# Batch 0 of a Fourier-mixing and mixture-of-experts kernel stays on chip between its stages

## The chip, the cores and the metric

The kernel runs on one core of one Trainium2 chip. The metric is the device time of one execution in microseconds (us), the median of several. A profile of one execution gives a span from the first to the last instruction, which is a little shorter than such a time. The engines are called TensorE (PE in the profile; PEld is its weight load), VectorE (DVE), ScalarE (ACT), GpSimd (POOL) and SyncE (SP, which here issues most transfers).

## What is computed

Two blocks follow each other, all in fp32. The first mixes each of 8 batches of 2496 x 256 along the sequence with a filter in the Fourier domain:

```python
X = np.fft.rfft(x, axis=1)
Y = X * (filt_r + 1j * filt_i)[None, :, :]
y = np.fft.irfft(Y, n=x.shape[1], axis=1)
```

The second takes the 19968 rows of y as tokens, sends each to the one expert of 8 with the largest logit, and scales the expert's result by the softmax weight of that expert:

```python
logits = x @ w_gate
expert_idx = np.argmax(logits, axis=1)
h = np.maximum(x_sorted[lo:hi] @ w1[e], 0.0)      # 256 -> 1024
y_sorted[lo:hi] = h @ w2[e]                        # 1024 -> 256
out = gate_w[:, None] * y_sorted[inv_perm]
```

No token is dropped, so the number of rows of each expert is known only at run time.

## The kernel before

**The Fourier block** splits 2496 = 39 x 64 and runs in four stages, each a set of small matmuls against a table. Stage A (`stage_a`, L324 to L335) transforms over the 39 with table `tas`; three columns of 39 make 117 partitions, and 22 such groups of columns are taken two at a time in chunks of four (`CH`). Its result z goes to DRAM (`zd`), because stage B needs the other index on the partitions. Stage B (`stage_b`, L337 to L354) transforms over the 64 for one pair of the 20 frequencies f with table `tbs`, and multiplies by the filter `ht` on VectorE with four operations (L350 to L353). Stage C (`stage_c`) goes back over the 64 with table `tcs`, and its result u goes through DRAM (`ud`) for the same reason. Stage D (`stage_d`, L377 to L391) goes back over the 39 with table `tds`, and leaves rows y.

**Routing.** `turn_y` transposes y, `logits` multiplies by `w_gate`, `turn_logits` transposes back, and `route` (L431 to L541), in three groups for each batch, finds the expert, and counts with two small matmuls into the PSUM tile `rk` (L467, L468) which row of the expert's list each token takes. GpSimd then scatters the rows to a list in DRAM (L526). `route` is a generator: each `yield` lets the main loop go on with something else.

**Experts.** `tile_map` reads from the counts which tiles of 512, 256 or 128 rows can be worked on. For each tile the rows are loaded (`xg`), transposed (`turn_x`), multiplied by `w1` (`hidden`, L663) with a ReLU, multiplied by `w2` (`result`, L677), scaled, and scattered to the output by GpSimd (L683).

**Order.** The order of the instructions on TensorE, VectorE, ScalarE and SyncE is written out by the kernel's own main loop, which keeps a clock `now` of planned costs. `slot(k)` lists the steps of one slot with a place between 0 and 1 for each: stages B and C of batch k, stage A of batch k+1, stage D and routing of batch k-1. Ahead of slot 0 stand stage A of batch 0 and the loads of the filter tables, in turn. After each step of the Fourier block the loop issues stores (`flush`) and loads that have room (`more_loads`, seven input buffers), and calls `side()` twice, each of which runs the routing to its next `yield`. Expert steps come in between when their data are planned to be there. `evac` copies a PSUM bank to SBUF on VectorE or ScalarE, whichever is planned to be free first; so all these copies have the line L231.

Each engine works in order: an instruction that waits holds up all that stand behind it on that engine.

Of the kernel before, what the change touches and what calls it, by code (L numbers as in the profile page):

```python
# [10 lines left out]
F32 = mybir.dt.float32  # L11
# [16 lines left out]
NF = (N1 + 1) // 2  # L28

NB = 3  # L30
NG = 22
TP = NB * N1
DH = D // P
# [3 lines left out]
def dft_tables():  # L37

    w = 2.0 * np.pi
    q = np.arange(N1)
    t = np.arange(N2)
    g = np.arange(N2)
    half = N2 // 2
    sg = np.where(g < half, 1.0, -1.0)  # L50

    ta = np.zeros((NB, N1, NB, N1))
    for f in range(NF):
        ang = w * ((q * f) % N1) / N1
        for j in range(NB):
            ta[j, :, j, f] = np.cos(ang)
            if f:
                ta[j, :, j, NF - 1 + f] = -np.sin(ang)

    tb = np.zeros((2, N2, NF, 2, N2))  # L60
    for f in range(NF):
        ang = w * ((t[:, None] * (f + N1 * g)[None, :]) % S) / S
        c, sn = np.cos(ang), np.sin(ang)
        if f:
            tb[0, :, f, 0] = c
            tb[1, :, f, 0] = sn
            tb[0, :, f, 1] = -sn * sg
            tb[1, :, f, 1] = c * sg
        else:
            tb[0, :, f, 0, :half] = c[:, :half]  # L70
            tb[0, :, f, 1, 1:half] = -sn[:, 1:half]
            tb[0, :, f, 0, half] = (-1.0) ** t

    tc = np.zeros((2, N2, 2, 2, N2))
    ang = w * ((g[:, None] * t[None, :]) % N2) / N2
    c, sn = np.cos(ang), np.sin(ang)
    tc[0, :, 1, 0] = c
    tc[0, :, 1, 1] = sn
    tc[1, :, 1, 0] = -sn * sg[:, None]
    tc[1, :, 1, 1] = c * sg[:, None]  # L80
    tc[0, :half, 0, 0] = 2.0 * c[:half]
    tc[1, :half, 0, 0] = -2.0 * sn[:half]
    tc[1, 0, 0, 0] = 0.0
    tc[0, 0, 0, 0] = 1.0
    tc[0, half, 0, 0] = (-1.0) ** t

    td = np.zeros((NB, N1, NG, NB, N1))
    ids = np.zeros((NB, N1, NG))
    valid = np.zeros((NB, N1, NG))
    for j in range(NB):  # L90
        for i in range(len(range(j, N2, NB))):
            n = N2 * q + NB * i + j
            ids[j, :, i] = n
            valid[j, :, i] = 1.0
            td[j, 0, i, j] = 1.0 / S
            for f in range(1, NF):
                ang = w * ((n * f) % S) / S
                td[j, f, i, j] = 2.0 / S * np.cos(ang)
                td[j, NF - 1 + f, i, j] = -2.0 / S * np.sin(ang)

    return {
        "ta": ta.reshape(TP, TP),
        "tb": tb.reshape(P, NF, P),
        "tc": tc.reshape(P, 2, P),
        "td": td.reshape(TP, NG, TP),
        "ids": ids.reshape(TP, NG),
        "valid": valid.reshape(TP, NG),
    }
# [24 lines left out]
def kernel(  # L133
# [37 lines left out]
    zd = [dram.tile([N2, N1, D], F32, tag=f"z{b % 2}", name="zd") for b in range(B)]  # L171
    ud = [dram.tile([N2, N1, D], F32, tag=f"u{b % 2}", name="ud") for b in range(B)]
# [13 lines left out]
    moe = ctx.enter_context(tc.tile_pool(name="moe", bufs=2))  # L186
# [7 lines left out]
    tas = cst.tile([TP, TP], F32, name="tas")  # L194
    tbs = cst.tile([P, NF, P], F32, name="tbs")
    tcs = cst.tile([P, 2, P], F32, name="tcs")
    tds = cst.tile([TP, NG, TP], F32, name="tds")
# [12 lines left out]
    tau_i = cst.tile([1, 64], I32, name="tau_i")  # L210

# [31 lines left out]
    def load_filters(c):  # L243
        f0, n = FH[c]
        nc.sync.dma_start(out=tbs[:, f0:f0 + n], in_=tb[:, f0:f0 + n])
        nc.sync.dma_start(out=ht[:, f0:f0 + n], in_=filt[:, f0:f0 + n, :])
        if c == 0:
            nc.sync.dma_start(out=ht[:, NF:], in_=filt[:, NF:, :])
            nc.sync.dma_start(out=tcs, in_=tcm)
# [28 lines left out]
    def columns(ap, i0, n):  # L278

        rows = ap.rearrange("t s d -> (t s) d")  # L280
        m = min(n, NG - 1 - i0)
        yield TP, slice(0, m), rows[i0 * TP:(i0 + m) * TP, :].rearrange("(i p) d -> p i d", p=TP)
        if m < n:
            yield N1, slice(m, n), rows[(NG - 1) * TP:, :].rearrange("(i p) d -> p i d", p=N1)
# [6 lines left out]
    def move(o, i):  # L291
        moves[1].append(lambda: nc.sync.dma_start(out=o, in_=i))
# [18 lines left out]
    def load_z(b, c):  # L311
        f0, n = FH[c]
        z0 = 1 if f0 == 0 else 0
        zi = fin(("z", b, c))
        nc.sync.dma_start(out=zi[:HP, :n], in_=zd[b][:, f0:f0 + n, :])
        nc.sync.dma_start(out=zi[HP:, z0:n], in_=zd[b][:, NF - 1 + f0 + z0:NF - 1 + f0 + n, :])
# [7 lines left out]
    def stage_a(b, c):  # L324
        i0, n = CH[c]
        xt = ins.pop(("x", b, c))
        zo = sb.tile([TP, 4, D], F32, tag="st", name="zo", bufs=4)
        for j in range(0, n, 2):
            p = bank()
            mm(p[:TP, :], lhsT=tas, rhs=xt[:TP, j:j + 2, :], start=True, stop=True)  # L330
            evac(zo[:, j:j + 2, :], p[:TP, :].rearrange("p (t d) -> p t d", t=2), 512)
        for r, m, v in columns(zd[b], i0, n):
            move(v, zo[:r, m])
        if c == len(CH) - 1:
            mark(("a", b))  # L335

    def stage_b(b, f):  # L337
        c, j = divmod(f, 4)
        zi = ins["z", b, c] if j == 0 else ins.pop(("z", b, c))
        p = bank()  # L340
        for i in range(2):
            k = HP if f + i == 0 else P
            mm(p[:, i * D:(i + 1) * D], lhsT=tbs[:k, f + i, :], rhs=zi[:k, j + i, :], start=True, stop=True)  # L343
# [9 lines left out]
        nc.vector.tensor_tensor(ys, ys, yw, op=ALU.add)  # L353
        free["v"] = max(free["v"], now[0]) + 2.8  # L354

    def stage_c(b, f):
# [12 lines left out]
        if j == 2:  # L369
            f0 = f - 2  # L370
            z0 = 1 if f0 == 0 else 0
            move(ud[b][:, f0:f0 + 4, :], uo[:HP])
            move(ud[b][:, NF - 1 + f0 + z0:NF - 1 + f0 + 4, :], uo[HP:, z0:])
# [3 lines left out]
    def stage_d(b, c):  # L377
# [4 lines left out]
        ui = ins.pop(("u", b, c))  # L382
        yo = outs["o", b, c] = sb.tile([P, 4, DR], F32, tag="y", name="yo", bufs=6)[:TP]
        for j in range(0, n, 2):
            p = bank()
            for i in range(2):

                k = N1 if i0 + j + i == NG - 1 else TP
                mm(p[:TP, i * D:(i + 1) * D], lhsT=tds[:k, i0 + j + i, :], rhs=ui[:k, j + i, :],  # L389
                   start=True, stop=True)  # L390
            evac(yo[:, j:j + 2, :D], p[:TP, :].rearrange("p (i d) -> p i d", i=2), 512)  # L391

# [38 lines left out]
    def route(b, g):  # L431
# [32 lines left out]
        yield  # L464
        rk = psr.tile([P, 2, E * NG], F32, tag="rk", name="rk")
# [78 lines left out]
    def tile_map(b, rows, n, last):  # L544

        av_i = moe.tile([1, E], I32, name="av_i", bufs=1)
        av = moe.tile([1, E], F32, name="av", bufs=1)
        end = moe.tile([1, E], F32, name="end", bufs=1)
# [9 lines left out]
        base = moe.tile([1, E], F32, name="base", bufs=1)  # L558
        add = moe.tile([1, E], F32, name="add", bufs=1)
# [6 lines left out]
        tau = moe.tile([1, n], F32, tag=f"tau{n}", name="tau", bufs=1)  # L566
        past = moe.tile([1, n, E - 1], F32, tag=f"past{n}", name="past", bufs=1)
# [5 lines left out]
        ef = moe.tile([1, n], F32, tag=f"ef{n}", name="ef", bufs=1)  # L573
        erow = moe.tile([1, n], I32, tag=f"erow{n}", name="erow", bufs=2)
# [4 lines left out]
        rf = moe.tile([1, n], F32, tag=f"rf{n}", name="rf", bufs=1)  # L579
        rrow = moe.tile([1, n], I32, tag=f"rrow{n}", name="rrow", bufs=2)  # L580
# [3 lines left out]
        if last:  # L584

            stop = moe.tile([1, 1], F32, name="stop", bufs=1)
# [5 lines left out]
        if not last:  # L592

            take = moe.tile([1, E], F32, name="take", bufs=1)
# [17 lines left out]
    def rows_in(i):  # L612
# [3 lines left out]
        xg = xgs[i] = moe.tile([P, 4, DR], F32, tag="xg", name="xg")  # L616
# [10 lines left out]
    def weights(h, second):  # L627
# [10 lines left out]
        if second:  # L638
            w2t[h] = moe.tile([P, FH2, D], F32, tag="w2t", name="w2t", bufs=3)
            nc.sync.dma_start(out=w2t[h], in_=moe_w2[bass.ds(ev, 1), k].rearrange("o p i d -> p (o i) d"))  # L640
        else:
            pool, bufs = (late["w1"], 8) if i >= SHORT else (moe, 3)
# [3 lines left out]
    def turn_x(i):  # L646
        n, xg = work[i][0], xgs.pop(i)
        idt[i] = moe.tile([P, 4, 1], I32, tag="idt", name="idt", bufs=3)
        gts[i] = moe.tile([P, 4, 1], F32, tag="gts", name="gts", bufs=3)
        nc.vector.tensor_copy(idt[i][:, :n], xg.bitcast(I32)[:, :n, D:D + 1])  # L650
        nc.vector.tensor_copy(gts[i][:, :n], xg[:, :n, D + 8:D + 9])
        xts[i] = moe.tile([P, DH, 4 * P], F32, tag="xT", name="xT", bufs=1)
# [6 lines left out]
    def hidden(i, k):  # L659
# [5 lines left out]
        hT = moe.tile([P, 512], F32, tag="hT", name="hT", bufs=9)  # L665
# [4 lines left out]
    def result(i, j):  # L670
# [7 lines left out]
        ys = moe.tile([P, D], F32, tag="ys", name="ys", bufs=4)  # L678
# [16 lines left out]
    def slot(k):  # L695

        steps, nch = [], len(CH)
        if k < B:
# [9 lines left out]
        if k > 0:  # L708
            for c in range(nch + 3):
                at = 0.2 + 0.8 * c / (nch + 3)  # L710
                if c < nch:
                    steps.append((at, lambda c=c: stage_d(k - 1, c), ("u", k - 1, c), 0.43 * CH[c][1]))
# [7 lines left out]
            steps.append((2.0, lambda: begin_route(k - 1), None, 0.0))  # L720
        return sorted(steps, key=lambda step: step[0])

    STEPS = []
    for c in range(len(CH)):
        STEPS.append((0.0, lambda c=c: stage_a(0, c), ("x", 0, c), 0.43 * CH[c][1]))
        if c < len(FH):
            STEPS.append((0.0, lambda c=c: load_filters(c), None, 0.0))
    STEPS.append((0.0, load_rest, None, 0.0))
# [12 lines left out]
    todo = [step[2] for step in STEPS if step[2]]  # L741
# [75 lines left out]
    with tc.manual_schedule(  # L817
# [8 lines left out]
        while f or e:  # L826
            asked = e and e[2] in when

            halt = f and f[2] and f[2][0] == "u" and held_y[0] == 6
# [5 lines left out]
            elif f and not halt and (not f[2] or f[2] in ins):  # L835
# [9 lines left out]
            side()  # L845
            side()
# [37 lines left out]
```

## Time and profile before

| what | value |
|---|---|
| time, median of 3 | 1698.14 us (1694.24 to 1699.72) |
| span of the profiled execution | 1670.8 us |
| mean granted TensorE clock | 0.974 |
| first stage-B matmul starts | 40.0 us |
| first stage-D matmul starts | 90.1 us |
| first expert matmul (L663) starts | 203.1 us |
| moved from and to DRAM | 299 MB, 179 GB/s over the span |

In the profile, L with a number is a line of the kernel. A group of instructions is written out<-in by the names in the program. A wait names the engine and the tile that waited, then what released it, then the total, the number of times and the longest in us. "issue" is time in which the profile shows nothing that the engine waited for. A matmul of fp32 appears as two records, one for each pass.

### The profile page before, as it was taken

The numbers are of one execution on the slowest core, as the hardware profiler recorded it, in microseconds if no ns is written. First come the engines' busy times: TensorE is split into PE (matmuls) and PEld (weight loads), VectorE is DVE, ScalarE is ACT, GpSimd is POOL, SyncE is SP. The second block draws the span as 40 slices with busy tenths as digits, with TensorE's granted clock in tenths as the row PEclk, the third lists the DMA queues.
The fourth block names the chain that finished last, engine by engine and source line by source line (L and its number), as shares of the span: only waits on it lengthen the run. The fifth ranks groups of instructions, "written<-read, shape, count | busy, mean of one in ns | idle before, by whom it ended". The sixth has DMA issues, their size and how long they took to land.

```text
span 1670.8 us, 21186 instructions
## 1 busy us (share of the span) xinstructions
PE 1574.8 (94%) x6886; PEld 1125.5 (67%) x6886; DVE 617.6 (37%) x1921; ACT 325.1 (19%) x608; POOL 344.3 (21%) x363
## 2 busy tenths in 40 slices
PE   3888798999999999999999989999999999999998
PEld 1454465677666666666676666676767668889997
DVE  0766776454632243233533332221101003334443
ACT  1333232121222222212222212212111110000000
POOL 0003322312410232021412221341111111111111
PEclk7899899999999999999999999999999999999999
DMA  8888887676673547434744353443344446565561
GB/s 318 272 242 266 255 265 239 205 256 184 213 244 115 168 154 231 150 121 126 197 134 129 121 160 101 129 152 121 109 158 143 145 140 224 190 207 174 176 189 47
DMA packets 125429, 299.53 MB, mean 179 GB/s; under 512 B 17681, under 2 KB 62874, under 8 KB 125075
## 3 DMA queue, kind: packets, MB, share of 16 engines
q1 hardware_dynamic: 106104, 254.85, 49.3%
q0 software_dynamic: 19216, 43.33, 7.6%
q8 instruction: 56, 0.92, 0.2%
q14 instruction: 53, 0.43, 0.1%
HBM read 213.91 MB, written 85.10 MB: 179 GB/s over the span
## 4 chain that ended last, share of the span: by engine, by line
PE 87%; DVE 6%; DMA 4%; issue 2%; ACT 0%; SPq 0%; POOLq 0%; POOL 0%; DVEq 0%; ACTq 0%
PE bank L677 33%; PE bank L663 33%; PE bank L389 4%; PE bank L330 3%; PE bank L367 3%; PE bank L343 3%; DMA zd<-zo 2%; PE bank L656 2%; PE bank L399 2%; PE lt L413 1%; DVE yw L352 1%; DVE yw L351 1%; DVE ys L350 1%; DVE ys L353 1%; DMA ud<-uo 1%
## 5 line engine op out<-in xcount | busy, mean ns | idle before, releaser
L663 PE MATMUL bank<-xT,w1t 128*128 128x512 f32 (+2 forms) x2080 | 590.9, 436 | 0.8 <-ACT xT L231 0.8
L677 PE MATMUL bank<-w2t,hT 128*128 128x256 f32 x2240 | 500.0, 380 | 0.0
L663 PEld LDWEIGHTS bank<-xT,w1t 128*128 128x128 f32 x2080 | 338.6, 191 | 203.7 <-issue 182.5
L677 PEld LDWEIGHTS bank<-w2t,hT 128*128 128x128 f32 x2240 | 423.3, 191 | 64.1 <-issue 9.4
L683 POOL DMA_INDIRECT out_dram<-ys,idt x163 | 159.5, 978 | 942.0 <-DVE ys L681 420.1
L526 POOL DMA_INDIRECT rows<-yo,row x176 | 175.4, 996 | 377.1 <-issue 225.5
L667 ACT ACTIVATE hT<-bank 128x512 f32<-128x512 f32 (+1 forms) x241 | 140.3, 582 | 494.2 <-PE bank L663 494.2
L681 DVE TENSOR_SCALAR ys<-bank,gts 128x256 f32<-128x256 f32 x145 | 70.1, 484 | 429.5 <-PE bank L677 429.5
L666 DVE TENSOR_SCALAR hT<-bank 128x128 f32<-128x128 f32 (+1 forms) x279 | 94.0, 337 | 70.2 <-PE bank L663 70.2
L343 PE MATMUL bank<-fin,tbs 128*128 128x256 f32 (+1 forms) x320 | 88.6, 399 | 23.6 <-issue 23.0
L330 PE MATMUL bank<-fin,tas 117*117 117x512 f32 x176 | 94.4, 665 | 6.0 <-DMA fin<-in_x_dram 5.9
L343 PEld LDWEIGHTS bank<-fin,tbs 128*128 128x128 f32 (+1 forms) x320 | 60.1, 198 | 55.9 <-issue 45.9
L389 PE MATMUL bank<-fin,tds 117*117 117x256 f32 (+1 forms) x352 | 88.7, 392 | 6.6 <-DMA fin<-ud 6.6
L231 DVE COPY xT<-bank 128x512 f32<-128x512 f32 (+2 forms) x59 | 28.3, 480 | 162.8 <-ACT hT L667 98.2
L350 DVE TENSOR_TENSOR ys<-bank,ht 128x512 f32<-128x512 f32 x80 | 55.0, 688 | 87.7 <-PE bank L343 86.3
L389 PEld LDWEIGHTS bank<-fin,tds 117*117 117x117 f32 (+1 forms) x352 | 64.5, 187 | 33.7 <-issue 14.0
L367 PE MATMUL bank<-ys,tcs 128*128 128x512 f32 x144 | 78.8, 630 | 8.0 <-DVE ys L353 8.0
L231 ACT COPY xT<-bank 128x512 f32<-128x512 f32 (+2 forms) x71 | 29.9, 431 | 284.3 <-PE bank L656 200.9
L677 PE MATMUL bank<-w2s,hT 128*128 x368 | 83.2, 379 | 0.0
L677 PEld LDWEIGHTS bank<-w2s,hT 128*128 128x128 f32 x368 | 68.2, 190 | 8.2
L231 ACT COPY uo<-bank 128x512 f32<-128x512 f32 x80 | 46.9, 586 | 119.3 <-PE bank L367 91.3
L330 PEld LDWEIGHTS bank<-fin,tas 117*117 117x117 f32 x176 | 35.0, 203 | 42.4 <-issue 37.5
(106 smaller groups left out, 852.0 us busy)
## 6 DMA issues: line engine op xcount, KB each, us to landing
w1t<-in_moe_w_dram SPq DMA_DIRECT2D x130, 512.0 KB
w2t<-in_moe_w_dram SPq DMA_DIRECT2D x84, 512.0 KB
fin<-in_x_dram SPq DMA_DIRECT2D x40, 512.0 KB
zd<-zo SPq DMA_DIRECT2D x40, 468.0 KB
fin<-ud SPq DMA_DIRECT2D x40, 468.0 KB
fin<-zd SPq DMA_DIRECT2D x72, 256.0 KB
ud<-uo SPq DMA_DIRECT2D x72, 256.0 KB
xg<-rows SPq DMA_DIRECT2D x28, 544.0 KB
```

The costliest lines, as they stand in the source:

```text
L231: either(n, lambda: nc.vector.tensor_copy(o, i), lambda: nc.scalar.copy(out=o, in_=i))
L330: mm(p[:TP, :], lhsT=tas, rhs=xt[:TP, j:j + 2, :], start=True, stop=True)
L343: mm(p[:, i * D:(i + 1) * D], lhsT=tbs[:k, f + i, :], rhs=zi[:k, j + i, :], start=True, stop=True)
L350: nc.vector.tensor_mul(ys, z2, ht[:, f:f + 2, :])
L367: mm(p, lhsT=tcs[:, 1, :], rhs=ys, start=True, stop=True)
L389: mm(p[:TP, i * D:(i + 1) * D], lhsT=tds[:k, i0 + j + i, :], rhs=ui[:k, j + i, :], start=True, stop=True)
L526: sc = nc.gpsimd.indirect_dma_start(out=rowsd, out_offset=bass.IndirectOffsetOnAxis(ap=at, axis=0), in_=what, in_offset=None,)
L663: mm(p[:, :m], lhsT=w1t[2 * i + k // FH2][:, dh, k % FH2 * P:(k % FH2 + 1) * P], rhs=xts[i][:, dh, :m], start=(dh == 0), stop=(dh == DH - 1))
L666: either(m, lambda: nc.vector.tensor_scalar_max(hT[:, :m], p[:, :m], 0.0), lambda: nc.scalar.activation(hT[:, :m], p[:, :m], AF.Relu))
L667: lambda: nc.scalar.activation(hT[:, :m], p[:, :m], AF.Relu))
L677: mm(p[:, :D], lhsT=hs[i][k][:, j * P:(j + 1) * P], rhs=w2, start=(k == 0), stop=(k == FT - 1))
L683: nc.gpsimd.indirect_dma_start(out=out, out_offset=bass.IndirectOffsetOnAxis(ap=idt[i].bitcast(U32)[:, j, :], axis=0), in_=ys, in_offset=None,
```

## The change

Batch 0 is the first through all stages, and nothing else is there to be done while it goes through DRAM. The changed kernel keeps it in SBUF. Stage A of batch 0 (`first_a`) has the data as the weights and the table as the moving operand, so that z comes out with the model dimension on the partitions; it is kept in the tile `zt`. `turn_z` transposes the part that stage B needs for a pair of frequencies. Stage C (`first_c`) does the same with the tile `ut`, and `turn_u` transposes ahead of stage D. These tiles lie in a pool `pro` whose memory is given to the experts' buffers once stage D of batch 0 is planned (`experts_pool`). For this a place is added so that z and u have 40 columns instead of 39 (`NS`), also for the other batches. For batch 0 the last of the four operations of stage B is given to GpSimd.

The filter tables are loaded ahead of all stores; the real part, which was loaded twice, once for each half of the partitions, is loaded once and copied on ScalarE. Stage D of batch 0 is placed early in slot 1. In `route` the rank product is placed ten yields later, and the main loop calls `side()` four times after a step.

```diff
+NS = 2 * NF
+TK = NB * NS
@@ load_filters
-        nc.sync.dma_start(out=ht[:, f0:f0 + n], in_=filt[:, f0:f0 + n, :])
+        nc.sync.dma_start(out=ht[:HP, f0:f0 + n], in_=filt[:HP, f0:f0 + n, :])
+        nc.sync.dma_start(out=ht[rows, NF + f1:NF + f1 + nh], in_=filt[rows, NF + f1:NF + f1 + nh, :])
@@ stage_b
-        zi = ins["z", b, c] if j == 0 else ins.pop(("z", b, c))
+        if b == 0:
+            zi, j = outs.pop(("zi", f)), 0
+        else:
+            zi = ins["z", b, c] if j == 0 else ins.pop(("z", b, c))
...
-        nc.vector.tensor_tensor(ys, ys, yw, op=ALU.add)
+        (nc.gpsimd if b == 0 else nc.vector).tensor_tensor(ys, ys, yw, op=ALU.add)
@@ stage_d
-        ui = ins.pop(("u", b, c))
+        ui = turn_u(c) if b == 0 else ins.pop(("u", b, c))
@@ new
+    def first_a(c):
+            zu["z"] = pro.tile([P, DH, NF, 2, N2], F32, name="zt", bufs=1)
+            zu["u"] = pro.tile([P, DH, N2, 2, NF], F32, name="ut", bufs=1)
+        for j in range(0, n, 2):
+            p = bank()[:, :4 * TK]
+            for h in range(DH):
+                for i in range(2):
+                    mm(p[:, (2 * h + i) * TK:(2 * h + i + 1) * TK], lhsT=xt[:TP, j + i, h * P:(h + 1) * P], rhs=tas,
+                       start=True, stop=True)
...
+            for h in range(DH):
+                evac(zv[:, h], pv[:, h], 2 * TK)
+    def turn_z(f):
+        if f % 4 == 0:
+            nc.scalar.copy(out=ht[HP:, f:f + 4], in_=ht[:HP, f:f + 4])
...
+                nc.tensor.transpose(p[:, i, h, :], zu["z"][:, h, f + i].rearrange("p c t -> p (c t)"), ident)
+        evac(zi, p.rearrange("p i h d -> p i (h d)"), 2 * D)
+    def first_c(f):
...
+                mm(p[:, h, i].rearrange("p c t -> p (c t)"), lhsT=ys[:, i, h * P:(h + 1) * P],
+                   rhs=tcs[:, min(f + i, 1), :], start=True, stop=True)
+        for h in range(DH):
+            evac(zu["u"][:, h, :, :, f:f + 2], p[:, h].rearrange("p i c t -> p t c i"), D)
+    def turn_u(c):
+        ui = pro.tile([P, 4, D], F32, tag="ui", name="ui", bufs=1)
...
@@ route
+        for _ in range(10):
+            yield
         rk = psr.tile([P, 2, E * NG], F32, tag="rk", name="rk")
@@ slot
+        if k == 0:
+            steps.append((0.4, load_rest, None, 0.0))
...
-                at = 0.2 + 0.8 * c / (nch + 3)
+                at = 0.45 * c / (nch + 3) - 0.1 if k == 1 else 0.2 + 0.8 * c / (nch + 3)
...
+                if k == 1 and c == nch:
+                    steps.append((at, experts_pool, None, 0.0))
-            steps.append((2.0, lambda: begin_route(k - 1), None, 0.0))
+            steps.append((0.34 if k == 1 else 2.0, lambda: begin_route(k - 1), None, 0.0))
@@ STEPS
+    STEPS = [(0.0, lambda c=c: load_filters(c), None, 0.0) for c in range(len(FH))]
+    STEPS += [(0.0, lambda c=c: first_a(c), ("x", 0, c), 0.43 * CH[c][1]) for c in range(len(CH))]
@@ main loop
-            side()
-            side()
+            for _ in range(4):
+                side()
```

## The prediction

> **What bounds the kernel now.** I read the page's busy times and slices first, then a table of six stretches, the waits of TensorE, the chain of waits of the first 50 us, and TensorE's timeline at two places.
>
> The page, engine totals, granted clock and DMA share in 40 slices:
>
> ```profile
> PE 1574.8 (94%) x6886; PEld 1125.5 (67%) x6886; DVE 617.6 (37%) x1921; ACT 325.1 (19%) x608; POOL 344.3 (21%) x363
> ...
> PE   3888798999999999999999989999999999999998
> ...
> PEclk7899899999999999999999999999999999999999
> DMA  8888887676673547434744353443344446565561
> ```
>
> TensorE is the bound of the whole, and what it loses lies at the left edge. The stretches:
>
> ```profile
> 0.00:40.00 40.00, 11.54 (x23) 4.67 (x23) 3.89 (x11) 4.80 (x7) 1.67 (x16) 0.74 0.86 317
> 40.00:120.00 80.00, 68.37 (x227) 38.98 (x228) 52.37 (x91) 25.94 (x47) 0.00 (x0) 0.91 0.90 265
> 120.00:203.00 83.00, 67.74 (x306) 41.70 (x305) 59.62 (x176) 26.54 (x52) 25.58 (x26) 0.89 0.84 262
> 203.00:340.00 137.00, 124.44 (x529) 85.07 (x530) 81.89 (x276) 35.60 (x71) 46.79 (x47) 0.95 0.76 238
> 340.00:1100.00 760.00, 738.04 (x3077) 506.97 (x3076) 273.22 (x860) 171.16 (x314) 184.75 (x187) 0.99 0.53 161
> 1100.00:1670.80 570.80, 564.70 (x2730) 448.09 (x2728) 146.60 (x510) 61.05 (x120) 85.47 (x88) 1.00 0.48 156
> ```
>
> Columns: stretch, length, busy time of PE, PEld, DVE, ACT, POOL, granted clock, DMA share, GB/s. TensorE idles 28.5 us before 40, 11.6 and 15.3 us up to 203 (where the first expert matmul runs), 12.6 us up to 340, 28 us in all the rest, most of it before 1100. Its waits:
>
> ```profile
> PE rk L467 <- DVE oe L459: 27.0, 12, 5.4
> PE bank L343 <- issue: 23.0, 1, 23.0
> PE rk L467 <- DVE sd L463: 9.6, 4, 2.9
> PE bank L367 <- DVE ys L353: 8.0, 8, 1.6
> PE bank L389 <- DMA fin<-ud: 6.6, 2, 5.1
> PE bank L330 <- DMA fin<-in_x_dram: 5.9, 2, 5.5
> PE rk L467 <- ACT yt L231: 5.2, 1, 5.2
> ```
>
> Two things make up two thirds of the 96 us of idle time: one wait of 23 us in front of the first stage-B matmul, and 41.8 us in front of the routing's rank product. The chain shows what the 23 us are:
>
> ```profile
> 5.46 5.53 PE bank L330 x8
> ...
> 11.78 9.60 DMA zd<-zo
> ...
> 22.07 17.92 issue
> 39.99 2.34 PE bank L343 x4
> ```
>
> Stage A ends at 17 us; the first B needs z of batch 0 back from DRAM. The stores stand behind 5.2 MB of filter tables and 1.2 MB of tds, and the loads of z are issued at 36.2 us. "issue" here is that round trip. The rank product, from TensorE's timeline:
>
> ```profile
> 190.47 0.65 PE L467 MATMUL rk<-oe,tri 117*117 117x64 f32 x2 [5.44 <-DVE oe L459]
> ```
>
> It is issued after 4 yields of the routing, at two a step; VectorE, in order, has stage B's four 0.69 us operations among the routing's small ones.
>
> [...] granted clock 0.50 in 20 to 40 us, 0.91 and 0.89 up to 203, 1.00 late. So idle time removed there is paid back a little more than once. [...] No GpSimd tensor_tensor is in this trace. [...]
>
> **The change, part by part.** Unit costs from TensorE's timeline at full clock: a 512-wide fp32 matmul 0.86 us, two of 256 the same, eight transposes 0.80 us, so 0.107 us a pass and 128 columns (the experts' passes of 128 columns, each with its own weight load, measure 0.117: 85.9 us over 736 records, so weight loads hide).
>
> 1. Batch 0 without DRAM. Removed: the store and load of zd and ud for batch 0, about 4 x 2.5 = 10 MB, and 1.3 MB of filter, of the 55 MB moved up to 203 us. Stage A of batch 0 becomes 44 matmuls of 120 columns, two passes each: 88 x 0.1 = 8.8 us, against 11 x 0.86 = 9.5. Stage C the same way: 40 x 2 x 0.107 = 8.6, as before. Added: 40 transposes for z (4.3 us) and 44 for u (4.7). The order of TensorE's instructions sums to 8.4 us more work in all (1503.5 against 1495.1 at full clock), which TensorE, being the bound, pays. At the start it fills holes.
>
> Copies: 22 for z and 20 for u at about 0.42 (DVE) or 0.38 (ACT), as the 128x256 rows of the trace, 10 + 11 of 512 at 0.69/0.59, and five 64x1024 copies of the filter at about 1.1 on ACT (its copies of 512 elements take 0.59). VectorE gives the last add of B to GpSimd in this batch[...]; GpSimd is idle then (0.00 busy from 40 to 120). Who waits for it is stage C, one step later (about 3 us)[...]. One step of slot 0 (two frequencies) is 0.43 transposes + 0.86 B + 0.86 C + about 0.95 of A for batch 1 = 3.1 us on TensorE; DVE has 2.07 + about 0.7, ACT about 2.5. TensorE still sets the pace. The copies into u write pairs of 8 bytes; if they take twice as long, ACT reaches about 3 us a step, level with TensorE. I take 1x, and keep 2x for the range.
>
> The time to the first D of batch 0: start 5.5, A to 17 as before (the x chunks arrive no faster), then 39.5 - 8.8 = 30.7 us of work at a clock of 0.92 = 33.4, fill and first waits about 6: 56 us. Before, this point was at 90.
>
> 2. From there to the first expert matmul: 80 us of work (before: 77.3 us took 113, from 90 to 203, of which 20 us idle, and the rest a low clock and gaps between groups). I allow 14 for clock and gaps, and 15 idle: six times 0.8 us where D waits for the copy of its single ui buffer, 5 of C waiting for VectorE, 3 of rank products, 2 for u of batch 1. Sum 109: the first expert matmul at 165 us instead of 203. Gain there 38 us. What is left after it is 9.8 us more than before (1384.1 against 1374.3).
>
> 3. Rank product ten yields later, sides called four times a step. Of the 41.8 us, 15 lie before 203 and are in step 2. Of the 26.7 later ones (6.4 + 5.2 + 11.2 + 3.9) I take 16 as gained. For it: waits are 1 to 3 us and the distance grows from 2 steps to 3.5, and the routing's first operations now stand together on VectorE without a stage B among them. Against it: the matmuls queued behind rk are C and D of the next step, and the load of u (wait of 5.1 us at 972 us) was partly hidden by rk's wait.
>
> 4. Order of the table loads, smaller filters: on SyncE ahead of all stores; all tables are in by about 20 us at the 317 GB/s seen there. Part of step 1, nothing of its own. The 40th column of z and u: 2.6% more of these bytes, at a DMA share of about 0.5 in the expert stages: hidden. The experts' buffers in the place of zt and ut: their first load follows the last transpose of u, at about 80 us, long before 165: nothing.
>
> Sum: 165 + 1467.7 (203.1 to the end, before) + 9.8 - 16 = 1626.5 against 1670.8: 0.9735. Times 1698.14 (the factor from span to time is 1.0164): **1653 us**.
>
> **Rivals.**
> (a) More: TensorE runs the first part nearly unbroken, first expert at 150, and 24 of the 26.7 us go: 150 + 1467.7 + 9.8 - 24 = 1603.5, that is 1630 us. For it: DVE was only 65 to 72% busy there, DMA load falls. Against: in-order VectorE had C waiting even before.
> (b) Less: strided copies at 2x and a slow GpSimd add make slot 0 bound by its copies, first expert at 185, and the rank waits turn into waits for u, 5 saved: 1657.5, that is 1685 us. For it: the u wait at 972, the unknown copies.
> (c) Slower: the first expert comes no earlier than 203, because batch 0's rows wait for the later rank product and its scatters (GpSimd 1 us each, 22 of them), and the other waits only move: 203 + 1467.7 + 9.8 = 1680.5, that is 1708 us. For it: 9.8 us of work certainly more, and the order puts about as much TensorE work ahead of the first expert (119.4 against 120.8 us). Against: between the last rank product of batch 0 and the first expert stand 28 us of TensorE work, and scatter, landing and load need about 21 (8 + 2 + landing and load some 10).
>
> **How the numbers follow.** Forecast 0.54, (a) 0.17, (b) 0.16, (c) 0.13. The likeliest gives 1653. The range takes in (a) and (b) with some room for both bounds of the copies, and leaves (c) out: 1622 to 1690. Faster: forecast, (a) and nearly all of (b), 0.85; the edge of (b) and (c) gives 0.03 for the same; slower 0.12.
>
> **What would show it.** Right: TensorE has no wait over 6 us between 17 and 60; first L405 near 56, first L745 near 165; rk waits under 15 in all; from the first expert on the span is 1455 to 1470 us[...]. Wrong: ut or zt copies over 0.7 us, C waiting for GpSimd, expert matmuls waiting for xg or w1t, or waits of L405 for ud that grew by what rk lost.

## The result and the profile after

The changed kernel takes 1656.9 us (median of 4, 1652.7 to 1657.6) against 1698.9 us of the kernel before beside it (1694.2 to 1700.9). The ratio is 0.975, with a 95% interval of 0.9725 to 0.9777: faster by 2.5%.

One thing must be known to read the numbers below. The experiments ran on three chips, and the kernel before takes 1695.0 us on the first and 1673.9 us on each of the other two. The chip of the result above is not on record; by its times it is the first, or one like it, and I count it so. The profile of before that the prediction reads (span 1670.8 us, time 1672.5) looks like the other two. So I compare kernels of one chip, or say where a comparison goes from the second chip to the third, and use for the first chip another profile of the kernel before, with a span of 1696.3 us.

The page of the changed kernel, totals and slices:

```profile
span 1651.0 us, 21615 instructions
...
PE 1573.7 (95%) x7094; PEld 1143.5 (69%) x7094; DVE 622.3 (38%) x1942; ACT 333.8 (20%) x625; POOL 359.7 (22%) x373
...
PE   6887799999899999999999989999999999999998
...
DMA  8648977697773567435653363443334437565551
```

The first digit of PE (the share of the first fortieth of the span in which TensorE is busy) goes from 3 to 6: stage B of batch 0 no longer waits for DRAM. The same six stretches as before, the last one shorter (length, busy PE, PEld, DVE, ACT, POOL, granted clock, DMA share, GB/s):

```profile
0.00:40.00 40.00, 24.55 (x132) 19.33 (x133) 11.40 (x27) 10.81 (x20) 4.21 (x18) 0.87 0.92 272
40.00:120.00 80.00, 68.45 (x376) 49.26 (x374) 50.23 (x100) 29.85 (x57) 18.40 (x16) 0.94 0.53 147
120.00:203.00 83.00, 62.74 (x260) 39.52 (x261) 56.62 (x166) 24.90 (x47) 22.03 (x22) 0.96 0.87 262
203.00:340.00 137.00, 127.40 (x550) 88.04 (x550) 83.47 (x273) 36.94 (x73) 40.57 (x41) 0.96 0.78 235
340.00:1100.00 760.00, 745.76 (x3118) 511.27 (x3117) 277.48 (x887) 175.48 (x319) 197.14 (x198) 0.99 0.56 168
1100.00:1651.00 551.00, 544.84 (x2665) 436.07 (x2664) 143.07 (x494) 55.80 (x111) 77.31 (x79) 1.00 0.47 155
```

TensorE's waits in it (us in total, times, longest):

```profile
PE bank L503 <- DVE ls L241: 12.4, 4, 4.0
PE bank L344 <- DMA fin<-in_x_dram: 10.7, 2, 9.2
PE bank L405 <- DMA fin<-ud: 8.7, 2, 6.2
PE bank L424 <- DMA fin<-in_x_dram: 5.4, 1, 5.4
PE bank L405 <- ACT ui L241: 4.2, 4, 3.3
PE bank L384 <- DVE ys L370: 3.8, 3, 1.5
PE bank L449 <- POOL ys L370: 3.2, 4, 1.7
PE rk L549 <- DVE oe L538: 2.4, 4, 1.3
```

The wait of 23 us in front of stage B is gone, and the waits for the rank product (rk) fell from about 42 to 2.9 us (2.4 here and one of 0.5). New are 9.2 us for rows of batch 1 (L344), the waits for ui (4.2 here and 2.3 further down the list), and 12.4 us in front of the transposes of the logits (L503). The first stage D starts at 69.1 us and the first expert matmul at 186.5.

### The profile page after: what moved, and what is told of

Read it like the earlier page. It is cut to its first block, busy times and chain, and to the rows that moved or that the text cites. A ratio compares the mean times of both kernels' runs of the same rounds, so it can differ in the third digit from the quotient of the medians.

```text
span 1651.0 us, 21615 instructions
## 1 busy us (share of the span) xinstructions
PE 1573.7 (95%) x7094; PEld 1143.5 (69%) x7094; DVE 622.3 (38%) x1942; ACT 333.8 (20%) x625; POOL 359.7 (22%) x373
## 4 chain that ended last, share of the span: by engine, by line
PE 88%; DVE 5%; DMA 4%; issue 1%; another core or an unknown queue 1%; ACT 1%; SPq 0%; POOL 0%; POOLq 0%; DVEq 0%; ACTq 0%
PE bank L745 34%; PE bank L759 34%; PE bank L405 4%; PE bank L344 3%; PE bank L359 3%; PE bank L384 3%; PE bank L738 2%; PE bank L478 2%; PE lt L492 1%; DMA zd<-zo 1%; DVE yw L368 1%; DVE yw L367 1%; DVE ys L370 1%; DVE ys L366 1%; DMA ud<-uo 1%
## 5 line engine op out<-in xcount | busy, mean ns | idle before, releaser
L241 DVE COPY xT<-bank 128x512 f32<-128x512 f32 (+2 forms) x61 | 29.1, 477 | 192.1 <-ACT hT L749 98.2
L405 PE MATMUL bank<-fin,tds 120*117 120x256 f32 (+1 forms) x308 | 79.3, 398 | 8.7 <-DMA fin<-ud 8.7
L344 PE MATMUL bank<-fin,tas 117*120 117x512 f32 x154 | 76.8, 619 | 10.7 <-DMA fin<-in_x_dram 10.7
L405 PEld LDWEIGHTS bank<-fin,tds 120*117 120x117 f32 (+1 forms) x308 | 57.7, 190 | 33.5 <-issue 16.9
L384 PE MATMUL bank<-ys,tcs 128*128 128x512 f32 x126 | 67.1, 615 | 8.4 <-DVE ys L370 3.8
L359 PE MATMUL bank<-fin,tbs 128*128 128x256 f32 x280 | 74.3, 389 | 0.0
L359 PEld LDWEIGHTS bank<-fin,tbs 128*128 128x128 f32 x280 | 52.8, 194 | 21.3 <-issue 15.8
L367 DVE SCALAR_TENSOR_TENSOR yw<-bank,ht 64x512 f32<-64x512 f32 x80 | 55.4, 692 | 1.1
L241 ACT COPY uo<-bank 128x512 f32<-128x512 f32 x70 | 41.0, 585 | 73.3 <-PE bank L384 48.9
```

Source lines behind the costliest of these rows:

```text
L241: either(n, lambda: nc.vector.tensor_copy(o, i), lambda: nc.scalar.copy(out=o, in_=i))
L344: mm(p[:TK, :], lhsT=tas, rhs=xt[:TP, j:j + 2, :], start=True, stop=True)
L359: mm(p[:, i * D:(i + 1) * D], lhsT=tbs[:, f + i, :], rhs=zi[:, j + i, :], start=True, stop=True)
L367: nc.vector.scalar_tensor_tensor(out=yw[:HP], in0=z2[HP:], scalar=-1.0, in1=fi, op0=ALU.mult, op1=ALU.mult)
L384: mm(p, lhsT=tcs[:, 1, :], rhs=ys, start=True, stop=True)
```

## The experiments

**The kernel before again, and the two halves of the change apart.** These ran on the first chip. One kernel is the kernel before unchanged:

> The kernel before once more, unchanged. Its profiled execution (span 1670.8 us) was 27 us shorter than the median of its other executions (1698.9), while the changed kernel's profiled execution (1651.0) is only 6 us shorter than its median. Theory A: the profiled execution of before was an unusual one, and in an ordinary one TensorE loses some 25 us more in waits of the first 350 us that the shown profile has not; then this run's profile has a span near 1697, with idle time of TensorE near 120 us instead of 96. Theory B: the kernel before is the same in every execution and the profiler changes it; then the span here is again near 1671 and the times near 1698.

It took 1695.3 us, ratio 1.0007 (0.9992 to 1.0023), and its profile has a span of 1696.3 us, with 108.5 us idle. So theory B is out, and of theory A only the span came true: the idle time is 12.5 us above the 96.0 of the first profile and not 24, and the other half of the difference is longer busy time (1587.8 against 1574.8 us), at a mean granted clock of 0.966 against 0.974. Nor was the first profile an unusual execution: the executions of the kernel before on this chip all take 1689 us or more, and its 1672.5 us is an ordinary time of the other two chips. The next kernel has only the later rank product:

```diff
+        for _ in range(10):
+            yield
         rk = psr.tile([P, 2, E * NG], F32, tag="rk", name="rk")
...
-            side()
-            side()
+            for _ in range(4):
+                side()
```

> The kernel before with the rank product ten yields later and four calls of the routing after a step, and nothing else of the change. Theory (two separate parts, the rank product worth as much as the start): the 41.8 us of waits for the rank product fall below 6, about half of it comes back as waits of the transposes of the logits and of C, so some 20 us faster, about 1678, ratio 0.988. Rival (the gain is batch 0 on chip, the rank waits only move): within 5 us of before. Second rival (the rank product is all of it): about 1657, ratio 0.975.

It took 1653.1 us, ratio 0.9752 (0.9718 to 0.9786): the whole gain. The waits for rk fell from 42.4 us (28.7, 9.6 and 4.1) to 11.2, not below 6:

```profile
PE rk L469 <- DVE oe L459: 8.4, 3, 4.7
...
PE rk L469 <- issue: 2.3, 1, 2.3
...
PE rk L469 <- DVE ls L231: 0.5, 1, 0.5
```

My own theory (0.988) fell, and the second rival stands. The third kernel is the changed one without these lines:

> The changed kernel with the rank product where it was and two calls of the routing after a step. Theory (two parts): waits for the rank product are back at 30 us or more, about 1677, ratio 0.987. Rival (the gain is batch 0 on chip): 1657 to 1662, ratio 0.976. Second rival (the rank product is all): 1690 or more.

It took 1693.2 us, ratio 0.9985 (0.9972 to 0.9999), with 35.3 us of waits for rk. Batch 0 on chip alone is worth 0.15%. Again the second rival.

Four stretch tables show where this comes from. The cuts are at the first stage D and the first expert matmul of each kernel; the columns are those of above. The kernel before:

```profile
0.00:92.20 92.20, 52.82 (x133) 26.11 (x133) 39.41 (x63) 20.02 (x34) 1.67 (x16) 0.84 0.85 280
92.20:209.30 117.10, 97.32 (x423) 61.33 (x423) 76.67 (x213) 37.72 (x72) 26.31 (x26) 0.86 0.85 254
209.30:1696.30 1487.00, 1437.68 (x6332) 1042.75 (x6332) 500.70 (x1646) 266.02 (x503) 317.25 (x322) 0.98 0.52 164
sum 1696.30, PE 1587.82 PEld 1130.19 DVE 616.78 ACT 323.76 POOL 345.22; mean PE 529.27 PEld 376.73 DVE 205.59 ACT 107.92 POOL 115.07
```

The rank product alone:

```profile
0.00:91.60 91.60, 55.05 (x132) 27.36 (x132) 39.18 (x63) 20.41 (x34) 1.67 (x16) 0.80 0.85 281
91.60:201.30 109.70, 93.83 (x422) 58.86 (x422) 75.66 (x213) 37.04 (x73) 27.84 (x28) 0.91 0.91 270
201.30:1652.30 1451.00, 1422.40 (x6332) 1036.34 (x6332) 499.32 (x1645) 267.12 (x504) 314.95 (x320) 0.99 0.53 168
sum 1652.30, PE 1571.28 PEld 1122.56 DVE 614.15 ACT 324.57 POOL 344.45; mean PE 523.76 PEld 374.19 DVE 204.72 ACT 108.19 POOL 114.82
```

The changed kernel:

```profile
0.00:69.10 69.10, 49.78 (x279) 39.21 (x279) 31.66 (x59) 25.18 (x47) 14.38 (x26) 0.91 0.83 237
69.10:186.50 117.40, 92.97 (x423) 59.71 (x423) 79.41 (x213) 37.19 (x71) 22.16 (x22) 0.95 0.69 200
186.50:1651.00 1464.50, 1430.97 (x6394) 1044.59 (x6394) 511.20 (x1671) 271.42 (x507) 323.12 (x325) 0.99 0.55 171
```

Batch 0 on chip alone:

```profile
0.00:69.00 69.00, 50.03 (x279) 39.42 (x279) 31.67 (x59) 25.16 (x47) 14.36 (x26) 0.91 0.82 236
69.00:196.60 127.60, 103.78 (x438) 66.11 (x437) 81.73 (x223) 38.60 (x73) 21.98 (x22) 0.89 0.67 202
196.60:1694.60 1498.00, 1446.80 (x6380) 1050.86 (x6380) 510.09 (x1661) 268.78 (x505) 322.08 (x325) 0.98 0.53 165
```

Read the rank product first, the two tables with sums. The same TensorE work takes 44.0 us less: 27.5 us less idle time (108.5 to 81.0) and 16.5 us less busy time. Most of the second part is the clock. In all these profiles the granted clock is either whole or half (0.50), and it is half for 114.9 us of the first profile and 83.7 us of the second. The mean clocks of 0.966 and 0.975 say the same: over the spans 57.7 and 41.3 us are lost. A part of that falls on idle time. Where TensorE was busy, the loss is 40.6 against 27.2 us, so 13.4 of the 16.5 us are the clock; the other 3.1 stay open. How the half clock lies at a wait, the profile of the prediction shows: the wait of 5.44 us for rk ends at 190.5 us, and the granted clock is 1.00 from 180.0 to 186.7 us, 0.50 from 186.7 to 196.9, and 1.00 again up to 203.0. A wait that was removed here took 1.6 times its length with it (44.0 to 27.5). Between the profile of the prediction and those of three kernels on the other two chips, which change only this place, the same quotient is 1.6, 2.1 and 2.2 (32.2 us of span to 19.8 of idle time, 26.7 to 12.5, 14.8 to 6.7), so there is no fixed price.

Now batch 0 on chip, again by comparing each kernel with its partner. With the late rank product (second and third table) the first stage D comes 22.5 us earlier, 7.7 us are given back before the first expert matmul, and 13.5 us after it: 1.3 us remain. Without it (first and fourth) the three are 23.2, 10.5 and 11.0 us: 1.7 remain. What is given back is of two kinds. With the late rank product it is 13.5 us more idle time and 7.7 us more busy time, without it 5.9 and 15.6. So neither new waits nor more work explains it alone. The additional work itself can be estimated with the clock taken out, as busy time less half of the busy time at clock 0.50: that is 1544.0 to 1547.2 us in the seven profiles with batch 0 through DRAM and 1553.9 to 1556.6 in the seven with batch 0 on chip, so about 10 us. On the third chip the three kernels were run again, beside each other:

> The changed kernel again, beside its two halves on one chip. The kernel before took 1695 to 1699 us in the first two comparisons and 1674 in the third, which ran on another chip. Theory: what differs is how often TensorE's clock is halved after its waits, so a kernel with fewer waits differs less between the chips. Where before takes 1674 the changed kernel takes 1634 to 1642, ratio 0.976 to 0.981; where it takes 1695 it takes 1653 to 1657 as before. Rival: the chips differ by one factor, and the ratio is 0.975 on both.

> The kernel before with the rank product placed later alone, again beside the changed kernel. Theory (keeping batch 0 on chip saves at the start what it adds in TensorE work): within 0.4% of the changed kernel on either chip. Rival (on the chip with 1674 us the halves are worth different amounts): slower than the changed kernel by 0.6% or more.

> The changed kernel with the rank product where it was. Theory: within 0.5% of the kernel before on either chip. Rival: faster by 0.8% or more where before takes 1674.

Before took 1673.9 us there. The changed kernel has a ratio of 0.9811 (0.9781 to 0.984), 1641.9 us, at the edge of the expectation; the rank product alone 0.9783 (0.9748 to 0.9818), 1638.6 us; batch 0 on chip alone 1.0017 (1.0008 to 1.0026). So on both chips the rank product is worth the whole gain and batch 0 on chip nothing, and the whole change is no faster than the rank product alone. The first of these theories, that the clock is what differs between the chips, is not borne out for the changed kernel: its profile here is 6.5 us shorter than that of the result, with 9.9 us less idle and 3.5 us more busy time.

**What makes the rank product cheaper.** Two kernels on the second chip change one of the two places each. The first calls the routing four times a step, without the yields:

```diff
-            side()
-            side()
+            for _ in range(4):
+                side()
```

> The kernel before with four calls of the routing after a step instead of two, and no yields added: the routing's VectorE operations stand together, and the rank product comes one step after them instead of two. Theory (the distance between the routing's operations and the product is what counts): rank waits grow from 42 to 50 us or more, about 1700, ratio 1.003 or more. Rival (it is the grouping that counts): rank waits below 25, ratio 0.985 or less.

The second has three yields and two calls, which is the same distance of 3.5 steps as in the changed kernel:

```diff
+        for _ in range(3):
+            yield
         rk = psr.tile([P, 2, E * NG], F32, tag="rk", name="rk")
```

> The kernel before with three yields added ahead of the rank product and two calls after a step: the product comes 3.5 steps after the routing's start, as in the changed kernel, but the operations are not grouped. Theory (distance counts): rank waits fall from 42 to below 20, ratio 0.985 or less. Rival (grouping counts as much): rank waits stay above 30, ratio 0.99 or more.

Four calls alone gave 0.9924 (0.9894 to 0.9954), where I had expected a loss, and the waits for rk fell to 29.2 us, so the theory fell; its rival had "below 25" and 0.985 or less, and fell too. Distance alone gave 0.9856 (0.9828 to 0.9884), with 22.7 us. Both together gave 0.9783 on the third chip, with 12.6 us. So distance counts for more, and four calls count too, by themselves and on top of it. That they count because the routing's operations stand together on VectorE is argued, not shown: four calls also bring the routing to its end earlier (the first expert matmul starts at 184.8 us, with distance alone at 197.6), and no run parts the two. The rival of the second had "stays above 30" and is out; the theory's "below 20" was missed by 2.7 us.

**The new wait of 9.2 us.** The timelines of the changed kernel, TensorE and SyncE's queue:

```profile
30.99 3.74 PE L344 MATMUL bank<-fin,tas 117*120 117x512 f32 x4 [9.16 <-DMA fin<-in_x_dram]
```

```profile
22.12 0.47 SPq L260 DMA_DIRECT2D ht<-in_filt_dram  x1
22.70 4.36 SPq L324 DMA_DIRECT2D fin<-in_x_dram  x5
```

The second chunk of rows of batch 1 is asked for at 22.7 us, behind the last filter table, though its place is free much earlier and the last tables are wanted much later. One experiment puts each later table after a step of stage A (first chip):

```diff
-    STEPS = [(0.0, lambda c=c: load_filters(c), None, 0.0) for c in range(len(FH))]
-    STEPS += [(0.0, lambda c=c: first_a(c), ("x", 0, c), 0.43 * CH[c][1]) for c in range(len(CH))]
+    STEPS = [(0.0, lambda: load_filters(0), None, 0.0)]
+    for c in range(len(CH)):
+        STEPS.append((0.0, lambda c=c: first_a(c), ("x", 0, c), 0.43 * CH[c][1]))
+        if c + 1 < len(FH):
+            STEPS.append((0.0, lambda c=c: load_filters(c + 1), None, 0.0))
```

> The changed kernel with the first chunk of filter tables ahead of stage A of batch 0 and each later chunk after one step of it, so that the rows of batch 1 are asked for before most tables. Theory: TensorE's wait of 9.2 us at 31 us for the rows of batch 1 falls below 2, and the first expert matmul comes 5 to 9 us earlier (186.5 before), so 1649 to 1652, ratio 0.971. Rival (the transfers of the first 30 us are the limit, so the wait moves to a filter table): the same wait behind another name, 1655 to 1659.

It took 1646.6 us, ratio 0.9703 (0.9675 to 0.9731), against 0.9751 (0.9725 to 0.9777) of the changed kernel. The wait fell from 9.2 to 1.1 us, the first stage D comes at 62.2 us instead of 69.1, and the first expert matmul at 182.1 instead of 186.5, 4.4 us earlier where 5 to 9 were expected. The theory holds for the wait; the two intervals still touch, so the gain in time rests on the next kernel as well. That one has a second buffer for ui in addition, on the second and on the third chip:

```diff
-        ui = pro.tile([P, 4, D], F32, tag="ui", name="ui", bufs=1)
+        ui = pro.tile([P, 4, D], F32, tag="ui", name="ui", bufs=2)
```

> The changed kernel with the filter tables between the steps of stage A, as in e3_tables_between, and in addition two buffers for the transposed u of batch 0 instead of one. Theory (keeping batch 0 on chip takes away the wait of 23 us and puts small new waits in its place, the single ui buffer being 6.5 us of them): waits in front of stage D and of the transposes of u fall from 6.5 to below 3, ratio 0.968 against 0.970 of e3_tables_between. Rival (what limits the way from the first stage D to the first expert matmul is VectorE's order, so the wait moves to C or to the transposes of the logits): ratio within 0.001 of e3_tables_between.

> The changed kernel with the tables between the steps of stage A and two ui buffers, beside the changed kernel itself. Theory (the wait of 9.2 us for the rows of batch 1 is the one thing of the start that can be mended): 0.3 to 0.6% faster than the changed kernel, best of all. Rival: within 0.2% of it.

The ratios are 0.9757 (0.9732 to 0.9783) and 0.976 (0.9731 to 0.979); on the third chip, beside the changed kernel, it takes 1632.8 against 1641.9 us. It is 0.55% faster than the changed kernel, and had the lowest median of the kernels on that chip. But the second buffer has no part in that which the profile shows. On the second chip its waits for ui are those of the changed kernel:

```profile
PE bank L405 <- ACT ui L241: 4.1, 4, 3.3
...
PE bank L464 <- DVE ui L241: 2.3, 1, 2.3
```

That part of the theory is out. What the buffer is worth in time, no two kernels on one chip show, because the kernel without it ran on the first chip alone. The longest of these waits has another cause, which ScalarE's timeline of the changed kernel shows:

```profile
91.77 0.26 ACT L529 ACTIVATE ex<-ex 117x64 f32<-117x64 f32 x1 [3.92 <-DVE ex L528]
91.93 1.06 ACT L241 COPY ui<-bank 120x512 f32<-120x512 f32 x2
```

The routing's exponential waits 3.92 us for VectorE, which has a stage B ahead of it; the copies of ui stand behind it on ScalarE, and stage D waits for them, up to 3.3 us. How these two would be placed better was not tried.

**The round trip without the chip.** The wait of 23 us might be the tables ahead of the stores, so that a better order would do what keeping batch 0 on chip does. This kernel has the late rank product, and batch 0 through DRAM (the diff leaves out the rank product, and that half of the filter's imaginary part is loaded with the third chunk):

```diff
-        if c < len(FH):
+        if c < 2:
             STEPS.append((0.0, lambda c=c: load_filters(c), None, 0.0))
-    STEPS.append((0.0, load_rest, None, 0.0))
...
+        if k == 0:
+            for c in range(2, len(FH)):
+                steps.append((4 * (c - 2) / (NF + 2) + 0.001, lambda c=c: load_filters(c), None, 0.0))
+            steps.append((0.6, load_rest, None, 0.0))
```

> The kernel before with the rank product placed later (as e1_rank_only, ratio 0.975), batch 0 still through DRAM, but only two chunks of filter tables ahead of its stores and loads; the other three chunks, half of the imaginary part and the table of stage D are loaded in slot 0. Theory (the wait of 23 us is the transfers in front of the round trip, not the round trip itself): the wait falls to about 12 us, ratio 0.969, as good as on chip with mended tables and without its 8.4 us of additional TensorE work. Rival (the round trip itself sets it, or the later tables make stage B wait instead): ratio 0.974 or more.

It took 1645.0 us on the second chip, ratio 0.9828 (0.9797 to 0.986): no faster than the rank product alone, which has 0.9783 (0.9748 to 0.9818) on the third. Its waits show where the time went:

```profile
PE bank L345 <- issue: 14.0, 1, 14.0
...
PE bank L369 <- DVE ys L355: 11.7, 8, 3.1
...
PE bank L345 <- DMA fin<-zd: 6.1, 2, 5.2
PE bank L345 <- DMA tbs<-in_tb_dram: 2.2, 1, 2.2
```

The wait fell from 23 to 14 us (about 12 were expected), and the first stage B came at 31.1 us, but the first stage D only at 98.2 (92.9 in the rank product alone, on the third chip). Stage B now waits 6.1 us for z and 2.2 for a table, and stage C 11.7 us for VectorE instead of 6.8. This fits tables that, moved into slot 0, compete with that slot's own transfers; no run shows it apart. The rival holds for this order; others were not tried.

## Why the prediction was right, and where it was not

The time was right: 1653 forecast, 1656.9 measured, inside the range. The reasons were not. The sum expected its gain from two parts, batch 0 on chip and the later rank product, and the runs give all of it to the second. The one term was too large by about as much as the other was too small, and that they cancelled is luck.

**Step 3 is the one that failed**, the later rank product. I took 16 of the 26.7 us of waits that lie after the first expert matmul and priced a wait at its own length, though I had written that removed idle time is paid back "a little more than once". Measured with this edit alone after the first expert matmul, on the first chip: 36.0 us (1487.0 to 1451.0), of which 20.7 us are idle time and 15.3 busy time, 13.5 of these by the clock. In this stretch the waits for rk fell from 27.4 to 4.2 us. The transposes of the logits took over 2 us of them, as I feared (5.4 to 7.4), stage D none (6.3 to 5.4).

**Steps 1 and 2 were too large.** I gave batch 0 on chip and the early rank waits together 38 us up to the first expert matmul, less 9.8 us of additional work. Measured against the kernel before on that chip: 22.8 us earlier (209.3 to 186.5), of which the rank product alone brings 8.0, and 13.5 us of the rest are given back afterwards. What I missed: stage A of batch 1 waits 9.2 us, because step 4 put the tables ahead of everything and called this "nothing of its own"; the first stage D came at 69 us instead of 56. From there to the first expert matmul I took 109 us and it was 117.4: the idle time is 24.4 us where I allowed 15. Waits for ui were 6.5 us against 4.8 allowed, and those in front of L503, for u, for xg and for x of batch 1 together 7.5, of which I had allowed 2 for u.

Of the signs that I had named, the waits for rk (2.9 us, under 15) and the span from the first expert matmul on (1464.5 us, 1455 to 1470) came as in the forecast; the start of stage D and "no wait over 6 us" did not. The first expert matmul started where rival (b) had put it (186.5 us, 185), though not for its reason. The additional work of 8.4 us was counted nearly rightly (about 10), and rival (c) named one reason why little came of the start: as much TensorE work stands ahead of the first expert matmul as before (with the clock taken out as above, 133.5 us against 133.4). GpSimd's add, which the profile of before does not have, took 1.27 us, and C waited 3.2 us for it in all. The copies into ut took 0.42 us on either engine (0.42 and 0.38 taken), so the copies at double length of rival (b) did not arise. The experts' buffers cost nothing that I could see: ahead of the first expert matmul TensorE waited 2.3 us for xg, and never for w1t.

The number also leaned on the factor from span to time, 1.0164, which I put on as if it held for every execution. In fact the profile read was that of an execution of 1672.5 us, about 26 us shorter than the timed ones. The forecast span was 1626.5 us, and the profile of the changed kernel has 1651.0. On the third chip, where the kernel before takes about what that profile says, the ratio is 0.9811 and not the 0.9735 forecast.

## What to carry to other kernels

In this kernel a small matmul that waits for a vector engine in the middle of a full TensorE queue cost 1.6 to 2.2 times its wait: price it with the clock that is half around it (13.4 of the 44.0 us above), and move it until what it needs is long done. Before work is moved on chip to save a round trip, ask what TensorE does in that time afterwards: here the same work stood ahead of the next stage (133.5 against 133.4 us), the transposes and the other additions (about 10 us by the estimate above) were paid, and of the 22.5 us by which the first stage D came earlier 1.3 us remained. When several edits come together, measure each alone: here two small edits to the order of the routing carried the whole gain.

## What was not expected of the hardware

The same kernel took 1695.0 us on one chip and 1673.9 on each of two others, with a mean granted clock of 0.966 to 0.975 in the executions on the first and 0.970 to 0.977 on the others. Why the chips differ is open, but the profiles have one trace of it. On the first chip VectorE or ScalarE sometimes waits for something that the profile cannot place, and lists as "remote". Such waits stand in all five profiles of the first chip and in none of the other nine, that of the prediction among them; in the changed kernel's they are two of VectorE with 9.0 us and one of ScalarE with 4.7.

In the changed kernel they lead to two of the four waits at L503. VectorE's copies of the logits, which these transposes need, themselves wait 5.0 and 3.9 us for such a release, and TensorE waits 3.5 and 4.0 us behind them. On the third chip the waits at this line sum to 5.8 instead of 12.4 us. What it is that they wait for stays open.

In the changed kernel the copies from PSUM to SBUF that turn the order of their elements and write pairs of 8 bytes (ut) took VectorE hardly longer: 422 ns in the mean for 128x256, against 419 for plain ones of that size (xT). On ScalarE they took 425 against 373.
